# Sixteen extra score products behind the last block of exponentials, one shared step less, and a different instruction for epsilon

## The chip, the core and the metric

The kernel runs on one core of a Trainium2 chip. The metric is device time in microseconds (us) of one execution. Five engines work side by side, each on its own queue in its own order: TensorE (PE, its weight loads PEld), VectorE (DVE), ScalarE (ACT), GpSimd (POOL) and SyncE (SP, which here issues the transfers).

## The reference

Four batches of 12480 queries attend through 49 agents, and the result goes through a feed-forward layer with a cosine in it:

```python
def sm(a, b):
    s = scale * (a @ b.transpose(0, 2, 1))
    s = s - s.max(-1, keepdims=True)
    e = np.exp(s)
    return e / (e.sum(-1, keepdims=True) + 1e-09)
agent_v = sm(agents, k) @ v
x = (sm(q, agents) @ agent_v).reshape(B * S, D)      # 49920 x 128
h = x @ w_in                                          # 128 -> 2048
out = (h * np.cos(h)) @ w_out                         # 2048 -> 128
```

## The kernel before, in words

Queries are taken in 52 groups of 960 (13 a batch). The main loop (from L1115) has 832 steps, 16 a group and 208 a batch. A step n is one pair of 128-row tiles of the hidden layer for 480 queries. PE makes the pair `ph` from the turned weights `pT` and the folded weights `a` (two matmuls); ACT takes the cosine, `c<-ph`; DVE makes `r = (c - 1) * h` in one scalar_tensor_tensor, `r<-c,ph`; PE multiplies `r` by w_out into `po` four steps later (LAG = 4, L36). PSUM holds three `ph` pairs, one bank `po`, and one bank `one` for everything else. So the matmuls of `ph(n)` can only run when `r(n-3)` has been made, and every tile in `one` waits until the tile before it has been read.

Inside a step the instructions are issued in this order, and each engine keeps it: `ph(n)` on PE, the cosine on ACT, what `plan` holds for the step (L1133), `r(n)` on DVE, what `post` holds for the step (L1151), then the two `po` matmuls of step n-4 on PE. In every eighth step two more matmuls (`po<-pT,b`) go ahead of those, and ACT copies `po` to `osb` afterwards.

Beside this, the softmax of the queries is made ahead: PE makes their scores in `one` (`one<-ag,xt`, eight products of 120 queries by the 49 agents, given twice, so 98 columns; a product in fp32 appears as two passes in the trace), ACT the exponentials, DVE and POOL the sums, DVE adds epsilon and takes the reciprocal (`query_inverse`, L734), POOL multiplies (`p<-e,rz`), PE turns the result (`query_turned`, L746: four transposes into `one`, which ACT copies to `p`), and POOL splits it into `pT`.

Exponentials need another table on ACT than the cosine, so they are gathered in bursts (`burst`, L994): ACT loads a table, runs the exponentials, and loads the sine table again. In the last batch the burst stands behind the cosine of step 720 (T3 = 96, L70) and holds the last four groups. The steps 720 to 723 are shut to other jobs. The sums of three groups and their inverse follow at once on DVE; the sum of the fourth is made on POOL behind step 724 and its inverse behind step 729. `query_turned` of group 46 stands in step 724, in `plan`. `keep_warm` (L989) already exists: four score products with columns of `win` as weights, into a new tile in `one` that nobody reads; a count FB of zero (L95) issues none.

`asides` (L1105) names steps in which DVE does only the first half of `r`: ACT copies the second half of `h` to `raw`, and POOL makes that half of `r` in two instructions. In the last batch these are the steps whose number is 0 or 8 modulo 16, except near a burst.

Of the kernel before, what the change touches and what calls it, by code (L numbers as in the profile page):

```python
# [14 lines left out]
ALU = mybir.AluOpType  # L15
# [10 lines left out]
EPS = 1e-9  # L26
# [27 lines left out]
SR = 4  # L54
# [15 lines left out]
T3 = 96  # L70
# [7 lines left out]
PJ = 1  # L78
QI = 5
KQ = [2, 0, 1, 4, 2, 3, 3, 3, 1, 5, 2, 4, 0]  # L80
VQ = [2, 3, 4, 3, 3, 3, 3, 3, 3, 3, 3, 3, 3]
# [10 lines left out]
RB = 6  # L92
OG = 0
VP = 1
FB = 0  # L95
FO = 0
TS = 1
VX = [5, 6, 7, 8]
DW = 2
# [1 line left out]
P2 = 0  # L101
BL = 6
XL = 16
XP = []
XK = [0, 8]
# [17 lines left out]
EQ = [0, 1, 2, 3, 4, 5, 6, 7, 8, 9, 10, 11, 12]  # L123
# [10 lines left out]
def agent_attention_cos_ffn(ctx, tc, qT, kT, v, agT, w_in, w_out, outT):  # L134
    nc = tc.nc
    NB, _, N = qT.shape
# [5 lines left out]
    DFF = w_in.shape[1] - PAD // 2  # L142
    NF = DFF // P
    NP = NF // 2
    NG = N // GRP
# [11 lines left out]
    PER = NG * STEP  # L157
# [19 lines left out]
    pe, dve, act, pool = (Ordered(x) for x in (nc.tensor, nc.vector, nc.scalar, nc.gpsimd))  # L177
# [250 lines left out]
    class Fast(Agents):  # L428
# [64 lines left out]
        def projected(self, c, a, pw):  # L493
            cs = slice(c * 512, (c + 1) * 512)
            if c == 0:
                self.big = self.sb.tile([KR, DFF // 512], F32, name="big", bufs=1)
            act.activation(a[:, cs], pw[:KR], AF.Copy, scale=self.rz)
            x = a[:, cs].bitcast(F32)
            on = dve if self.wide else pool
            on.tensor_scalar(a[:, cs], x, 2 * FAST_MAX, -2 * FAST_MAX, op0=ALU.min, op1=ALU.max)  # L500
            if self.wide and BL:
                late_big.append((self, c, x))
            else:
                self.largest(c, x)
# [91 lines left out]
    with ExitStack() as pools:  # L596
# [15 lines left out]
        a = []  # L612
# [120 lines left out]

        def query_inverse(piece, i, j):  # L734
            rz = rz_of[piece][:, i * GT:j * GT]
            dve.tensor_scalar_add(rz, rz, EPS)
            dve.reciprocal(rz, rz)

        def query_weights(n, on=pool):
# [28 lines left out]
        ab = [Fast(sb, small, b) if b else First(sb, small, b, pair) for b in range(NB)]  # L768
# [5 lines left out]
        first = ab[0]  # L774
# [3 lines left out]
        def convert(n):  # L778

            for f in words[:n]:  # L780
                f()
            del words[:n]
# [59 lines left out]
        def wide_kept(n, ps):  # L842
            mx = sb.tile([TT, GT], F32, name="mx4", bufs=3)
            mh = mx.rearrange("p (h t) -> p h t", h=2)
            if QM == 0:
                dve.reduce_max(mh, ps, axis=AX.X)
                dve.tensor_sub(e_of[n].rearrange("p (h t) a -> p h t a", h=2), ps,
                               mh.unsqueeze(3).to_broadcast([TT, 2, HT, NA]))
                return
            dve.reduce_max(mh, ps, axis=AX.X)  # L850
            dve.tensor_scalar_mul(mx, mx, -SC)
            for h in range(2):
                for t in range(HT):
                    i = h * HT + t
                    act.activation(e_of[n][:, i], ps[:, h, t], AF.Exp, bias=mx[:, i:i + 1], scale=SC)
# [18 lines left out]
        piece = pieces[0]  # L874
# [48 lines left out]
            pe.matmul(po_v[:TT, :DC], qx[2][:, :TT], qx[2][:, :DC], start=True, stop=True)  # L923
        for n in range(3):
            wide_kept(n, outs[n])
        for g in range(NG):
            fetch_to(VL[g])
            shift(g + AH)
            if g + AH < NG:
                first.exp(g + AH, 1)  # L930
            first.add(g, dve if g in EQ else pool)
            first.values(g)
            convert(VQ[g])
            for c in range(4):
                if g == TQ[c]:
                    turn(c)
                if g == MQ[c]:
                    mult(c)
            if g == TW - 1 and QM == 0:
                for n in piece:  # L940
                    act.activation(e_of[n], e_of[n], AF.Exp, scale=SC)
            if g == TW:
                for n in piece:
                    query_sum(n)
                query_inverse(piece, 0, len(piece))
                query_weights(0, dve if PA else pool)
            if g == TR:
                query_turned(0, PA)
            if g == TI:
                first.total()  # L950
                first.inverse()
        sine_table()
        first.gather()
        if TI == NG:
            first.total()
            first.inverse()
        for c in range(4):
            if MQ[c] == NG:
                convert(len(words) if c == 3 else 0)
                mult(c)  # L960
# [10 lines left out]
        plan, post = Plan(), Plan()  # L971
# [22 lines left out]
        def burst(n, piece, two=(), ab=None, also=()):  # L994

            shut.update(range(n, n + SHUT))
            wide_at.update(range(n, n + SHUT + WX))
            for i in range(0, len(two), 2):
                post(n + i // 2 * BD, query_two, two[i:i + 2], piece_of[two[0]])
            if ab is not None:  # L1000
                for g, k in lots:
                    post(n, pinned_exp, ab, g, k)
            post(n, query_exp, piece)
            if also:
                post(n, query_exp, also)
                post(n + 12, query_sums, also, 0, len(also))
                post(n + 20, query_inverse, also, 0, len(also))
            s0 = SF if ab is not None else SD1
            for k in piece[:s0]:
                post(n, query_sum, k)  # L1010
            post(n, query_inverse, piece, 0, s0)
            m = n + SM
            if ab is not None:
                for k in piece[s0:]:
                    post(m, query_sum, k)
                    m += 1
                post(m, query_inverse, piece, s0, len(piece))
                return
            for i in range(s0, len(piece), ST):
                j = min(i + ST, len(piece))  # L1020
                post(m, query_sums, piece, i, j)
                m += 1
            post(m + SR, query_inverse, piece, s0, len(piece))

        for c in range(max(1, P2), DFF // 512):
            plan(PJ * (c - max(1, P2)), ab[0].project, c, a[0])
        def big_late():
            late_big[0][0].largest(*late_big.pop(0)[1:])
        if BL:
# [17 lines left out]
        for b in range(NB):  # L1047
            o = b * PER
            go, stop = o + (T1 if b < NB - 1 else T3), o + PER + T2
            last = OG and b == NB - 2  # L1050
            if OG and b == NB - 1:
                break
            k0 = o + (T2 + K0 if b else KB)
            spread_over(k0 + (QS if b < NB - 1 else 0), go - 5, go - 1, [q_lot(n) for n in early[b][N2 if b else N0:]])
            if b == NB - 1:
                burst(go, early[b])
                for i in range(FB):
                    post(go + FO, keep_warm)
                break
            nxt = ab[b + 1]  # L1060
            spread_over(k0, o + K1, o + K1 + 1, [[(nxt.scores, g, k) for k in range(2)] for g in range(NG)])
            plan(o + K1 + 2, nxt.top)
            job(o + K1 + 4, (nxt.across,), by=o + K1 + 5)
            job(o + K1 + 6, (nxt.spread,), by=o + K1 + 8)
            for g in range(NG):
                plan(o + K1 + 9 + SH * g, nxt.shift, g, 1, pool)
            burst(go, early[b], late[b][:N1], nxt)
            for g in range(0, NG, VP):
                at = go + V0 + (o + V1 - go - V0) * g / NG
                job(at, *((nxt.values, x, k) for x in range(g, min(g + VP, NG)) for k in range(2)), by=at + 6 * VP)  # L1070
            spread_over(go + QV, o + V1 + 8 if last else stop - 3, o + V1 + 8 if last else stop - 1, [q_lot(n) for n in late[b][N1:]])
            if last:
                spread_over(o + V1 + 6, stop - 1, stop - 1, [q_lot(n) for n in early[b + 1][:-2]])
                burst(stop, late[b], early[b + 1][-2:], also=early[b + 1])
            else:
                burst(stop, late[b], early[b + 1][:N2])
            i = (b + 1) % 2
            job(o + V1 + 3, (nxt.inverse,), by=o + V1 + 8)
            job(o + V1 + 6, *((nxt.project, c, a[i]) for c in range(DFF // 512)), by=o + PER - 6)
            job(o + V1 + 7, (nxt.project_out, wio, b1[i], b2[i]), by=o + PER + 2)  # L1080
# [8 lines left out]
        while queue or begun:  # L1089
# [7 lines left out]
            n, i, by, parts = x  # L1097
# [7 lines left out]
        def asides(n):  # L1105

            b, o = n // PER, n % PER
            if n < XA or n > NSTEP - 6 or any(x in shut for x in range(n - XB, n + XC)):
                return False
            if b == NB - 1:  # L1110
                return n % XL in XK
            return X0 <= o < X1 and n % XL in XP

        rs = {}
        for n in range(NSTEP + LAG):  # L1115
# [3 lines left out]
            if n < NSTEP:  # L1119
                q, c, i = n // STEP, n // NP % NCH, n % NP  # L1120
# [209 lines left out]
```

## Time and profile before

| what | us |
|---|---|
| median of three runs | 1174.71 (1174.52 to 1177.32) |
| the profiled execution | 1173.36 |
| its span, first to last instruction | 1171.6 |
| mean granted TensorE clock | 0.996 of full |

The span is 1.8 us shorter than the profiled execution's own time, which is 1.35 us under the median. In the profile, PE is TensorE's matmuls and PEld its weight loads. A row of the timeline merges neighbouring instructions of one kind (x is their count); in brackets is the idle time ahead of it and what ended it. Shapes are partitions x elements. Granted clock 1.00 is 2.4 GHz, 0.50 is 1.2 GHz.

### The profile page before, as it was taken

The numbers are of one execution on the slowest core, as the hardware profiler recorded it, in microseconds if no ns is written. First come the engines' busy times: TensorE is split into PE (matmuls) and PEld (weight loads), VectorE is DVE, ScalarE is ACT, GpSimd is POOL, SyncE is SP. The second block draws the span as 40 slices with busy tenths as digits, with TensorE's granted clock in tenths as the row PEclk, the third lists the DMA queues.
The fourth block names the chain that finished last, engine by engine and source line by source line (L and its number), as shares of the span: only waits on it lengthen the run. The fifth ranks groups of instructions, "written<-read, shape, count | busy, mean of one in ns | idle before, by whom it ended". The sixth has DMA issues, their size and how long they took to land.

```text
span 1171.6 us, 17200 instructions
## 1 busy us (share of the span) xinstructions
PE 1123.6 (96%) x6051; PEld 918.3 (78%) x6051; DVE 1063.3 (91%) x1202; ACT 979.4 (84%) x1268; POOL 566.7 (48%) x727
## 2 busy tenths in 40 slices
PE   9989999999999999999999999999999999989996
PEld 8869888778886898777887788877888667767774
DVE  5878888989998988989999998998999999989997
ACT  3567877889888878898888888898988999989996
POOL 2013313668963212639893331175896456545551
PEclk9999999999999999999999999999999999999998
DMA  8734333143331333133331333214331100000001
GB/s 327 306 125 134 117 119 102 51 138 106 106 105 51 102 116 104 51 102 106 106 106 52 96 105 104 91 45 138 106 98 59 35 18 34 34 18 34 17 34 38
DMA packets 31631, 109.44 MB, mean 93 GB/s; under 512 B 3504, under 2 KB 4016, under 8 KB 31536
## 3 DMA queue, kind: packets, MB, share of 16 engines
q1 hardware_dynamic: 31392, 108.13, 28.4%
q8 instruction: 50, 0.82, 0.3%
q14 instruction: 45, 0.37, 0.1%
q10 hardware_dynamic: 144, 0.12, 0.0%
HBM read 82.68 MB, written 25.56 MB: 92 GB/s over the span
## 4 chain that ended last, share of the span: by engine, by line
PE 60%; DVE 21%; ACT 13%; issue 5%; DMA 1%; POOL 0%; SPq 0%; ACTq 0%; DVEq 0%
PE ph L171 26%; PE po L171 22%; DVE r L171 15%; PE one L171 12%; ACT c L171 7%; ACT osb L171 1%; DVE rz L171 1%; ACT e L171 1%; ACT p L171 1%; ACT s L171 1%; DVE sums L171 1%; DVE e L171 1%; ACT L171 1%; DVE mx L171 1%; DMA c<-kT 1%
## 5 line engine op out<-in xcount | busy, mean ns | idle before, releaser
L171 DVE SCALAR_TENSOR_TENSOR r<-c,ph 128x960 fp32r<-128x960 f32 (+1 forms) x833 | 906.1, 1133 | 41.8 <-ACT c L171 35.3
L171 ACT ACTIVATE c<-ph 128x960 f32<-128x960 f32 x832 | 785.4, 977 | 140.5 <-PE ph L171 126.3
L171 PE MATMUL ph<-pT,a 113*128 113x480 f32 x1664 | 520.9, 394 | 21.6 <-DVE r L171 16.9
L171 PE MATMUL po<-r,w 128*128 128x480 f32 x1664 | 524.2, 396 | 5.6 <-ACT osb L171 5.4
L171 PEld LDWEIGHTS ph<-pT,a 113*128 113x128 f32 x1664 | 294.6, 189 | 137.5 <-DVE r L171 73.3
L171 PEld LDWEIGHTS po<-r,w 128*128 128x128 f32 x1664 | 292.6, 190 | 52.0 <-ACT osb L171 14.1
L171 POOL CAST pT<-p 49x480 fp32r<-49x480 f32 x102 | 59.4, 582 | 266.7 <-ACT p L171 263.9
L171 PEld LDWEIGHTS one<-ag,xt 128*120 128x120 f32 x1088 | 133.9, 184 | 12.0 <-DVE sums L171 1.4
L171 PE MATMUL one<-ag,xt 128*120 128x98 f32 x1088 | 134.4, 265 | 0.4 <-DVE b L171 0.2
L171 POOL TENSOR_TENSOR pT<-p,pT 49x480 fp32r<-49x480 f32 x102 | 124.3, 1219 | 8.2
L171 POOL TENSOR_TENSOR vh<-vt,vh 120x512 fp32r<-120x512 f32 x78 | 93.4, 1198 | 30.5 <-ACT vh L171 30.5
L171 POOL TENSOR_TENSOR p<-e,rz 120x392 f32<-120x392 f32 x51 | 43.7, 856 | 47.6 <-DVE rz L171 46.3
L171 PE MATMUL po<-pT,b 113*128 113x480 f32 x208 | 62.5, 381 | 0.0
L171 POOL TENSOR_TENSOR raw<-c,raw 128x480 f32<-128x480 f32 x24 | 29.6, 1231 | 67.5 <-ACT raw L171 67.4
L171 POOL TENSOR_TENSOR e<-e,mx 120x392 f32<-120x392 f32 x25 | 21.2, 847 | 84.7 <-DVE mx L171 84.7
L171 ACT COPY osb<-po 128x480 f32<-128x480 f32 x104 | 57.9, 557 | 2.2 <-PE po L171 2.2
L171 PEld LDWEIGHTS ph<-ag,xt 128*120 128x120 f32 x480 | 52.0, 185 | 7.3 <-DVE r L171 4.4
L171 PE MATMUL ph<-ag,xt 128*120 128x98 f32 x480 | 54.4, 269 | 2.7 <-DVE r L171 2.0
L171 PEld LDWEIGHTS one<-vh,eh 120*113 120x113 f32 x312 | 45.9, 177 | 8.3 <-POOL vh L171 2.5
L171 PE MATMUL one<-vh,eh 120*113 120x258 f32 x312 | 50.7, 284 | 1.4 <-DVE e L171 1.4
L171 POOL TENSOR_TENSOR eh<-s,eh 120x196 fp32r<-120x196 f32 x78 | 47.7, 612 | 6.3
L171 POOL CAST eh<-s 120x196 fp32r<-120x196 f32 x78 | 27.7, 355 | 32.7 <-ACT s L171 32.3
(135 smaller groups left out, 730.7 us busy)
## 6 DMA issues: line engine op xcount, KB each, us to landing
xt<-qT SPq DMA_DIRECT2D x52, 480.0 KB, 3.6
outT<-osb SPq DMA_DIRECT2D x51, 480.0 KB, 2.6
xt<-kT SPq DMA_DIRECT2D x46, 480.0 KB, 3.6
vt<-v SPq DMA_DIRECT2D x43, 512.0 KB, 3.7
c<-kT SPq DMA_DIRECT2D x6, 480.0 KB, 7.4
vh<-v SPq DMA_DIRECT2D x5, 512.0 KB, 6.7
raw<-w_in SPq DMA_DIRECT2D x2, 512.0 KB, 6.6
a<-w_in SPq DMA_DIRECT2D x2, 512.0 KB, 6.4
```

Of the source, the lines that this page charges most:

```text
L171: ins = f(*args, **kw)
```

## The change

New constants: FB = 4 and FO = 4 put four `keep_warm` behind step 720 + 4 of the last batch, 16 products, 32 passes in the trace. XZ = 12 takes the steps 720 to 731 out of `asides`; 720 was already out, being in the burst, so this is step 728 alone. EP = 1 makes `query_inverse` add epsilon by a scalar_tensor_tensor, max(rz + EPS, rz), in place of a tensor_scalar; it is called 17 times. The other new constants (AL, CV, SZ, TN, GF, PO, PK, BM) have the values at which their branches issue the same instructions in the same order as before: SZ equals SR, and TN equals TI.

```diff
-FB = 0
-FO = 0
+FB = 4
+FO = 4
+SZ = 4
+XZ = 12
+EP = 1
...
         def query_inverse(piece, i, j):
             rz = rz_of[piece][:, i * GT:j * GT]
-            dve.tensor_scalar_add(rz, rz, EPS)
+            if EP:
+                dve.scalar_tensor_tensor(rz, rz, EPS, rz, op0=ALU.add, op1=ALU.max)
+            else:
+                dve.tensor_scalar_add(rz, rz, EPS)
             dve.reciprocal(rz, rz)
...
             if b == NB - 1:
-                return n % XL in XK
+                return n % XL in XK and not T3 <= o < T3 + XZ
```

What issues the extra products was there already, in the setup of the last batch:

```python
burst(go, early[b])
for i in range(FB):
    post(go + FO, keep_warm)
```

## Rows read from the trace of the kernel before

**Rows 1.** The page: busy us of an engine, share of the span, instructions.
```profile
PE 1123.6 (96%) x6051; PEld 918.3 (78%) x6051; DVE 1063.3 (91%) x1202; ACT 979.4 (84%) x1268; POOL 566.7 (48%) x727
```
**Rows 2.** The page: the chain that ended last, shares by engine.
```profile
PE 60%; DVE 21%; ACT 13%; issue 5%; DMA 1%; POOL 0%; SPq 0%; ACTq 0%; DVEq 0%
```
**Rows 3.** Windows: stretch and its us, busy PE, PEld, DVE, ACT, POOL, clock, DMA.
```profile
1038.20:1041.78 3.58, 0.01 (x1) 0.00 (x0) 2.01 (x5) 3.55 (x5) 0.00 (x0) 1.00 0.00 0
1042.50:1045.90 3.40, 3.40 (x12) 2.91 (x12) 2.50 (x4) 2.51 (x4) 1.71 (x2) 0.50 0.36 145
...
1060.00:1160.00 100.00, 97.71 (x415) 71.91 (x414) 95.74 (x93) 95.07 (x121) 49.65 (x48) 1.00 0.08 33
```
**Rows 4.** Timeline of PE behind the last burst: start, us, engine, instruction.
```profile
1037.17 0.60 PE L171 MATMUL po<-pT,b 113*128 113x480 f32 x2
...
1041.78 0.71 PE L171 MATMUL ph<-pT,a 113*128 113x480 f32 x2 [3.58 <-DVE r L171]
...
1042.33 0.84 PE L171 MATMUL one<-ident,p 120*113 120x120 f32 x4
```
**Rows 5.** Timeline of ACT behind the last burst.
```profile
1043.44 0.60 ACT L171 COPY p<-one 113x480 f32<-113x480 f32 x1
1044.82 0.97 ACT L171 ACTIVATE c<-ph 128x960 f32<-128x960 f32 x1 [0.78 <-PE ph L171]
```
**Rows 6.** The chain in order of time: start, us, what, instructions merged.
```profile
1043.17 0.81 PE po L171 x2
1043.98 0.80 PE ph L171 x2
...
1047.11 0.44 PE po L171 x2
```
**Rows 7.** Timeline of PE in a step with eight score passes.
```profile
987.55 0.98 PE L171 MATMUL one<-ag,xt 128*120 128x98 f32 x8
988.32 0.68 PE L171 MATMUL po<-r,w 128*128 128x480 f32 x2
```
**Rows 8.** Timeline of DVE behind the last burst, and one later period.
```profile
1045.82 1.15 DVE L171 SCALAR_TENSOR_TENSOR r<-c,ph 128x960 fp32r<-128x960 f32 x1 [0.90 <-ACT c L171]
1047.27 2.87 DVE L171 SCALAR_TENSOR_TENSOR r<-c,ph 128x960 fp32r<-128x960 f32 x3 [0.29 <-ACT c L171]
1050.36 1.16 DVE L171 SCALAR_TENSOR_TENSOR r<-c,ph 128x960 fp32r<-128x960 f32 x1 [0.22 <-ACT c L171]
1051.43 0.28 DVE L171 TENSOR_SCALAR rz<-rz 120x8 f32<-120x8 f32 x1
...
1068.32 8.46 DVE L171 SCALAR_TENSOR_TENSOR r<-c,ph 128x960 fp32r<-128x960 f32 x8 [0.22 <-ACT c L171]
```
**Rows 9.** Tile rz: count, least/median/most ns, first and last start.
```profile
L171 DVE TENSOR_SCALAR rz<-rz x17: 172/178/875, 50.3 to 1051.4; 120x24 f32<-120x24 f32 x13, 120x32 f32<-120x32 f32 x3, 120x8 f32<-120x8 f32 x1
```
**Rows 10.** Timeline of POOL and DVE, one slow epsilon of three like it.
```profile
254.41 1.20 POOL L171 TENSOR_TENSOR pT<-p,pT 49x480 fp32r<-49x480 f32 x1
254.78 0.87 DVE L171 TENSOR_SCALAR rz<-rz 120x24 f32<-120x24 f32 x1
```
**Rows 11.** Groups of DVE by form: count, busy us, mean ns, idle before.
```profile
L171 DVE SCALAR_TENSOR_TENSOR r<-c,ph 128x960 fp32r<-128x960 f32 x807 | 889.2, 1149 | 38.6 <-ACT c L171 35.3
...
L171 DVE SCALAR_TENSOR_TENSOR r<-c,ph 128x480 fp32r<-128x480 f32 x26 | 16.9, 654 | 3.1 <-ACT raw L171 0.7
...
L171 DVE TENSOR_SCALAR rz<-rz 120x24 f32<-120x24 f32 x13 | 4.4, 337 | 0.3
...
L171 DVE TENSOR_SCALAR rz<-rz 120x32 f32<-120x32 f32 x3 | 1.0, 338 | 0.0
```
**Rows 12.** Timeline of POOL and DVE in the first part.
```profile
50.98 1.20 POOL L171 TENSOR_TENSOR p<-e,rz 120x392 f32<-120x392 f32 x1 [43.29 <-DVE rz L171]
51.40 1.21 DVE L171 TENSOR_TENSOR s<-s,mxb 120x392 f32<-120x392 f32 x1
```
**Rows 13.** Tile s, 0 to 70 us: count, least/median/most ns.
```profile
L171 DVE TENSOR_TENSOR s<-s,mxb x13: 552/560/1206, 31.6 to 58.8; 120x392 f32<-120x392 f32 x13
```

More of the change, by code (lines that the diff above doesn't have):

```diff
@@ L94 @@
 VP = 1
-FB = 0
-FO = 0
+FB = 4
+FO = 4
+AL = 0
+CV = 0
+SZ = 4
+XZ = 12
+TN = 12
+GF = 1
+PO = 0
+PK = 0
+BM = 0
+EP = 1
 TS = 1
@@ L500, in projected @@
             on.tensor_scalar(a[:, cs], x, 2 * FAST_MAX, -2 * FAST_MAX, op0=ALU.min, op1=ALU.max)
-            if self.wide and BL:
+            if BL if self.wide else BM:
                 late_big.append((self, c, x))
@@ L925, in agent_attention_cos_ffn @@
             wide_kept(n, outs[n])
+        added = 0
         for g in range(NG):
@@ L930, in agent_attention_cos_ffn @@
                 first.exp(g + AH, 1)
-            first.add(g, dve if g in EQ else pool)
+            while added < min(NG, g + 1 + (AL if g else 0)):
+                first.add(added, dve if added in EQ else pool)
+                added += 1
             first.values(g)
-            convert(VQ[g])
+            if not (CV and g == NG - 1):
+                convert(VQ[g])
             for c in range(4):
@@ L950, in agent_attention_cos_ffn @@
                 first.total()
+            if g == TN:
                 first.inverse()
         sine_table()
-        first.gather()
+        if GF:
+            first.gather()
         if TI == NG:
             first.total()
+        if TN == NG:
             first.inverse()
+        if not GF:
+            first.gather()
+        if CV:
+            convert(VQ[NG - 1])
         for c in range(4):
@@ L1022, in burst @@
                 m += 1
-            post(m + SR, query_inverse, piece, s0, len(piece))
+            post(m + (SR if n < T3 + (NB - 1) * PER else SZ), query_inverse, piece, s0, len(piece))
         for c in range(max(1, P2), DFF // 512):
-            plan(PJ * (c - max(1, P2)), ab[0].project, c, a[0])
+            (post if PO >> c & 1 else plan)(PJ * (c - max(1, P2)) + (PK >> c & 1), ab[0].project, c, a[0])
         def big_late():
@@ L1052, in agent_attention_cos_ffn @@
                 break
+            if BM and b:
+                for c in range(DFF // 512):
+                    post(o + BM + 3 * c, big_late)
             k0 = o + (T2 + K0 if b else KB)
```

## The prediction
> **What bounds the kernel now.** I read the page first: PE is busy for 96% of the span [rows 1], but the chain that ended last gives PE only 60% and DVE 21% [rows 2]. So a busy PE is not yet the engine that sets the pace, and the pace has to be read stretch by stretch. The change touches two kinds of places: the stretch behind the last burst, and the 17 calls that add epsilon.
>
> The windows of that stretch come next [rows 3]. From 1038.20 to 1041.78 PE does nothing: ACT has loaded its table, run four exponentials and loaded the sine table again, and is making the first cosines, while the three `ph` pairs wait to be read. Then PE resumes at full clock, and from 1042.5 to 1045.9 it runs at the granted clock 0.50 (1.2 GHz); outside this stretch the clock is full until the end of the computation. PE is 100% busy in the slow stretch, DVE and ACT are not: 2.50 and 2.51 of 3.40 us. Here PE is the bound. Later, from 1060 to 1160, PE, DVE and ACT are all busy for over 95%, and nothing that was lost can be made up.
>
> The timeline says where in PE's order the new passes come. The matmuls `po<-pT,b` at 1037.17 belong to product step 719, issued in loop step 723, so the `ph` that waited 3.58 us and started at 1041.78 is that of step 724 [rows 4]. Behind it stand the four transposes of `query_turned`, which are in `plan` of step 724. The new passes are in `post` of the same step: behind both, ahead of `po(720)` and of `ph(725)`.
>
> **The 32 passes.** A removed or added instruction on PE between 1041.78 and 1046 moves the end, since DVE and ACT wait for `ph` there: ACT's cosine of step 725 waited 0.78 us for it [rows 5], and DVE's `r(725)` then 0.90 us for the cosine [rows 8].
>
> First their start. They write into `one`, which the transposes have filled and which ACT's copy to `p` reads from 1043.44 to 1044.04 [rows 5]. Before, PE went on at 1043.17 with `po(720)` [rows 6]; now it waits until 1044.04, and 0.04 more for the signal, 0.91 us in all, with `po(720)` and `ph(725)` queued behind.
>
> Then their length. Eight passes of the same shape took 988.32 - 987.55 = 0.77 us [rows 7], 0.096 us each at full clock; 32 take 3.08 us. At the slow clock a pair of matmuls took 0.81 us where it takes 0.44 later [rows 6], a factor of 1.8, so 0.175 us a pass. I take the slow stretch to end where it ended before, at 1045.9: (1045.90 - 1044.08) / 0.175 = 10.4 passes in it, and 21.6 x 0.096 = 2.07 us for the rest, until 1047.97. Then `po(720)` and `ph(725)`, 0.44 us each [rows 6] and 0.02 to ACT: the cosine of step 725 starts at 1048.87 instead of 1044.82 [rows 5], 4.05 us later. DVE's `r(725)`, next in line, starts as much later, at 1049.87.
>
> What comes back: the second gap of DVE in the slow stretch, 0.29 us [rows 8], since everything behind is at full clock. The first gap, 0.90 us, is only replaced by a longer one. Nothing is ahead of time that could take up the rest: DVE has made `r(724)` by 1044.92, 0.90 us ahead of `r(725)` [rows 8], and has no other work whose turn has come, as its next small job stands behind `r(729)`. Together 4.05 - 0.29 = +3.76 us.
>
> Bounds of this term: all passes at full clock end at 1044.08 + 3.08 = 1047.16, which is 0.81 us less, +2.95; all at half clock end at 1044.08 + 5.6 = 1049.68, and `po(720)` and `ph(725)` then take 0.8 us each [rows 6]: the cosine at 1051.3, 6.5 us later, less the gap +6.2. I take the middle because PE works on after its resumption as it did before, except for the 0.91 us.
>
> **The step that is no longer shared.** In step 728 DVE now makes the whole of `r`. The stretch with that step took 2.87 us for two whole and one half, and 0.22 us of idle time followed, in which DVE waited for a cosine [rows 8], because ACT's copy had delayed it: 3.09 us for three steps. Eight steps with one shared one take 8.46 + 0.22 = 8.68 us [rows 8], 1.085 a step, so three whole steps take about 3.26: +0.17 us. Bounds: +0.5 us if the idle time stays (654 ns against 1149 ns [rows 11]), and 0 if sharing saves nothing, as 1.085 a step already suggests. POOL and ACT lose three instructions that nobody was waiting for. One of them, POOL's product for the shared half, stood in the way of epsilon at 1051.43, which took 0.28 us [rows 8] instead of 0.17 [rows 9]: -0.10 us.
>
> **Epsilon by another instruction.** Undisturbed, the tensor_scalar takes 172 to 178 ns [rows 9]. A scalar_tensor_tensor of 24 elements isn't in the trace. From the two lengths of `r`, (1149 - 654) / 480 = 1.03 ns an element and a fixed 159 ns [rows 11], so an estimate of 184 ns: no difference that counts, 0.1 us over all 17.
>
> What could count is the disturbed ones. At 254.78 epsilon took 0.87 us; it started while POOL was at `pT<-p,pT` and ended with it [rows 10]. The form of 24 elements sums to 13 x (337 - 178) = 2.07 us of such waiting (three calls of 0.69) and that of 32 to 3 x (338 - 174) = 0.49 us [rows 11]. That is 2.56 us, and all of it lies between two `r` on DVE without a gap, so it is on the path.
>
> Does the new instruction escape it? The nearest row is a DVE instruction with two tensor inputs in SBUF: `s<-s,mxb` at 51.40 came while POOL ran `p<-e,rz`, and took 1.21 us [rows 12] where its median is 0.56 [rows 13]. The `r` instructions, which have one input in PSUM, don't stretch beside POOL. The new instruction reads `rz` twice, both from SBUF, so I count its wait like that of `s<-s,mxb`: 0 gained. The other end is -2.56 us. The row is of another operation and of two different tensors, so it does not settle it. The Trainium skill (SBUF — State Buffer, Who interferes with whom) says it in general: a DVE instruction with two SBUF inputs contends with a GpSimd instruction that reads SBUF, and the second to issue blocks until the first is done. By that rule the exchange gives nothing, and the sum is the one below; an instruction that escaped would be a rival.
>
> **The sum.** +3.76 + 0.17 - 0.10 + 0.1 = +3.9 us, made against the profiled execution: 1173.36 becomes 1177.3. That execution is 1.35 us under the median of the runs, to which I add the same: 1174.71 + 3.9 = 1178.6 us.
>
> **The rivals.**
>
> Slow clock stays on. PE now stands still for 0.91 us inside the slow stretch, and all the passes run at 1.2 GHz. For it: the clock fell at 1042.5, after 3.58 us in which PE did nothing [rows 3]. Against it: 0.91 us is far less, and no other stretch of the main loop with short PE gaps lost the clock. By the upper bound +6.2 + 0.2 = +6.4: 1181.1 us.
>
> Epsilon escapes POOL. The four long waits go: 3.9 - 2.56 = +1.3, 1176.0 us. For it: reading one tensor twice isn't what [rows 12] shows. Against it: both reads are from SBUF all the same.
>
> The passes fall into PE's idle time, the other side. If they ran ahead of `ph(724)`, they would use 3.08 of the 3.58 us in which PE had nothing to do [rows 3, 7]; they would cost nothing, PE would not have stood still, and with a full clock the gaps of 0.90 and 0.29 us [rows 8] would go: -1.2 + 0.2 = -1.0, 1173.7 us. It is decided by whether the first pass starts before 1041.78. For it: the passes fit. Against it: by the order of issue they stand behind `ph(724)`, which itself waits for `r(721)`, and behind transposes whose tile they need.
>
> **How the numbers follow.** No change is less than 0.3%, 3.5 us, about what a measurement can tell here; the three runs alone lie 2.8 us apart. My forecast has 0.48; since 3.9 us is just above the bound, 0.33 of it counts as slower and 0.15 as the same. The slow clock that stays has 0.16, all slower. Epsilon that escapes has 0.21, of it 0.19 the same and 0.02 slower. Idle time used has 0.10: 0.06 the same and 0.04 faster. The other 0.05 I give to things not thought of, all faster. Together faster 0.09, same 0.40, slower 0.51. The range goes from a little below the escaping epsilon, 1174.8, to the slow clock that stays, 1181.2; it leaves out the idle time used and what was not thought of.
>
> **What would show it.** In the changed kernel's timeline: passes `one<-ag,win` on PE that start only after ACT's copy to `p`, some 2.3 us after the first `ph` behind the burst; an idle PE of about 0.9 us ahead of them; the cosine of step 725 almost 5 us behind the end of that copy; a slow stretch of about 3.4 us as before; epsilon as a scalar_tensor_tensor with three calls still at 0.8 us or more; no copy `raw<-ph` in step 728. I am wrong if the first pass stands ahead of the `ph` that waited, if the long epsilons are gone, or if DVE's gap behind `r(724)` is under 3 us.

## The result, and the profile after

The changed kernel takes 1183.62 us (median of 10 runs, 1181.21 to 1186.97); the kernel before, run beside it, 1176.08 us (10 runs, 1173.67 to 1180.12). The ratio is 1.0069, 95% interval 1.0057 to 1.0082: slower by 8.1 us (0.0069 x 1176.08), where 3.9 was forecast and 1181.2 was the top of the range. The direction was right, the size was not.

The two profiled executions differ by more, 1185.21 - 1173.36 = 11.85 us. I split them at three instructions of DVE: `r(0)`, the first `r` of the main loop; `r(721)`, the first behind the last burst; and `r(737)`, behind the next shared half step.

| stretch | before, us | after, us | difference |
|---|---|---|---|
| start to r(0) | 73.54 | 77.18 | +3.64 |
| r(0) to r(721) | 967.03 | 967.18 | +0.15 |
| r(721) to r(737) | 19.08 | 27.14 | +8.06 |
| r(737) to the end of the span | 111.9 | 111.9 | 0.0 |

The 8.06 us are the change. The 3.64 us are not: they lie in the setup, where the change touches one epsilon of 0.2 us, and they go with a fall of the clock there that some traces have and others lack (experiment e11). The kernel before happened to be profiled without that fall, the changed one with it; this is why the two profiles differ by more than the medians.

The windows of the changed kernel show the places: us, then busy time of PE, PEld, DVE, ACT, POOL, the granted clock, DMA.

```profile
67.20:77.40 10.20, 8.33 (x19) 4.81 (x20) 1.93 (x8) 2.94 (x5) 0.00 (x0) 0.50 0.24 97
1041.99:1045.57 3.58, 0.00 (x1) 0.01 (x1) 2.02 (x5) 3.55 (x5) 0.00 (x0) 1.00 0.00 0
1046.81:1057.05 10.24, 9.00 (x36) 8.05 (x37) 1.89 (x2) 1.02 (x2) 6.43 (x12) 0.50 0.13 50
...
1064.00:1164.00 100.00, 97.70 (x413) 71.53 (x412) 95.75 (x94) 95.10 (x121) 48.34 (x46) 1.00 0.08 30
```

The idle time behind the burst is the same 3.58 us, and from 1064 on everything is as before [rows 3]. But the stretch at 1.2 GHz lasts 10.24 us where it lasted 3.4, and DVE and ACT are busy for 1.89 and 1.02 us of it.

PE's timeline, to be held against [rows 4] and [rows 6], shows the passes where the order of issue put them:

```profile
1045.57 0.70 PE L181 MATMUL ph<-pT,a 113*128 113x480 f32 x2 [3.58 <-DVE r L181]
1046.10 0.58 PE L181 MATMUL one<-ident,p 120*113 120x120 f32 x4
1047.88 7.86 PE L181 MATMUL one<-ag,win 128*120 128x98 f32 x32 [1.20 <-ACT p L181]
1055.44 1.15 PE L181 MATMUL po<-r,w 128*128 128x480 f32 x2
1056.38 0.91 PE L181 MATMUL ph<-pT,a 113*128 113x480 f32 x2
```

They wait 1.20 us for ACT's copy of the transposes, start 2.31 us behind the first `ph`, and `po(720)` starts 7.56 us later. The weight loads and the chain in order of time show stops inside: each new tile begins with one, and the tiles follow each other every 1.98 us.

```profile
1049.86 1.68 PEld L181 LDWEIGHTS one<-ag,win 128*120 128x120 f32 x8 [0.30 <-PE one L181]
```
```profile
1047.88 1.93 PE one L181 x8
1049.81 0.04 issue
1049.86 1.94 PE one L181 x8
```

DVE's timeline, against [rows 8], shows what that costs:

```profile
1044.36 4.35 DVE L181 SCALAR_TENSOR_TENSOR r<-c,ph 128x960 fp32r<-128x960 f32 x4 [1.49 <-ACT c L181]
1058.34 5.41 DVE L181 SCALAR_TENSOR_TENSOR r<-c,ph 128x960 fp32r<-128x960 f32 x5 [9.64 <-ACT c L181]
1063.67 0.16 DVE L181 SCALAR_TENSOR_TENSOR rz<-rz 120x8 f32<-120x8 f32 x1
...
1071.50 5.53 DVE L181 SCALAR_TENSOR_TENSOR r<-c,ph 128x960 fp32r<-128x960 f32 x5 [0.22 <-ACT c L181]
```

The gap ahead of `r(725)` is 9.64 us instead of 0.90: 8.74 us. Of these 0.68 come back up to `r(737)`: among others the gap of 0.29 us is gone, and epsilon, now undisturbed, takes 0.16 us. Epsilon elsewhere, against [rows 9] and [rows 11]:

```profile
L181 DVE SCALAR_TENSOR_TENSOR rz<-rz x17: 159/184/878, 50.7 to 1063.7; 120x24 f32<-120x24 f32 x13, 120x32 f32<-120x32 f32 x3, 120x8 f32<-120x8 f32 x1
```
```profile
L181 DVE SCALAR_TENSOR_TENSOR rz<-rz 120x24 f32<-120x24 f32 x13 | 4.4, 342 | 0.3
```

The longest still takes 878 ns, and three of the 13 take 0.87 us or more; the mean of 13 went from 337 to 342.

### The profile page after: what moved, and what is told of

Same layout as the page of the kernel before. It is cut to its first block, busy times and chain, and to the rows that moved or that the text cites. A ratio compares the mean times of both kernels' runs of the same rounds, so it can differ in the third digit from the quotient of the medians.

```text
span 1183.4 us, 17259 instructions
## 1 busy us (share of the span) xinstructions
PE 1135.0 (96%) x6083; PEld 926.5 (78%) x6083; DVE 1063.3 (90%) x1202; ACT 979.4 (83%) x1267; POOL 564.2 (48%) x725
## 4 chain that ended last, share of the span: by engine, by line
PE 60%; DVE 20%; ACT 13%; issue 4%; DMA 1%; POOL 0%; SPq 0%; ACTq 0%; DVEq 0%
PE ph L181 27%; PE po L181 21%; DVE r L181 15%; PE one L181 12%; ACT c L181 7%; DVE rz L181 2%; ACT osb L181 1%; ACT p L181 1%; ACT e L181 1%; DVE e L181 1%; DVE sums L181 1%; DMA c<-kT 1%; DVE mx L181 1%; ACT s L181 1%; DMA xt<-qT 1%
## 5 line engine op out<-in xcount | busy, mean ns | idle before, releaser
L181 PEld LDWEIGHTS po<-pT,b 113*128 113x128 f32 x208 | 38.7, 188 | 6.0
```

What stands on the lines that cost most here:

```text
L181: ins = f(*args, **kw)
```

## The experiments

All edits are to the changed kernel, except e2. For each I read the gap ahead of `r(725)` on DVE (0.90 us before, 9.64 in the changed kernel), the stretch at 1.2 GHz behind the burst (3.4 and 10.2), and the time from `r(721)` to `r(737)` against the 19.08 us before, worked out from the starts of those two in DVE's timeline. These hold whatever the setup did in that run.

| kernel | gap, us | slow stretch, us | r(721) to r(737), against before | ratio of times (95%) |
|---|---|---|---|---|
| the change | 9.64 | 10.2 | +8.06 | 1.0069 (1.0057 to 1.0082) |
| e1, no passes | 0.70 | 3.4 | -0.33 | 0.9992 (0.9977 to 1.0006) |
| e2, passes alone | 9.82 | 13.7 | +9.35 | 1.0072 (1.0047 to 1.0097) |
| e3, passes a step earlier | 0.18 | none | -0.34 | 0.9992 (0.9978 to 1.0005) |
| e4, 8 passes | 3.78 | 6.8 | +2.73 | 1.0014 (0.9999 to 1.0029) |
| e5, 16 long matmuls | 9.35 | 10.2 | +7.77 | one run |
| e6, ahead of the transposes | 9.23 | 13.7 | +8.50 | one run |
| e9, passes in one tile | 7.07 | 6.8 | +5.49 | one run |
| e10, long ones in one tile | 7.35 | 6.8 | +5.77 | one run |

**e1, no passes.**
```diff
-FB = 4
+FB = 0
```


> The changed kernel without the 32 passes; epsilon by the new instruction and step 728 whole, as in the change. Theory A (the passes are the whole loss): 0.998 to 1.002 of before; behind the burst the start of r(725) is where it was before, and r(737) within 0.4 us of it. The four long epsilons stay at 0.65 to 0.88 us. Theory B (the new epsilon or the step costs part of the loss): 1.002 or more, and the distance between the two kernels' r grows at an epsilon or between steps 726 and 737.

Ratio 0.9992. DVE's timeline and the window of its slow stretch:
```profile
1044.30 4.35 DVE L181 SCALAR_TENSOR_TENSOR r<-c,ph 128x960 fp32r<-128x960 f32 x4 [1.49 <-ACT c L181]
1049.35 1.16 DVE L181 SCALAR_TENSOR_TENSOR r<-c,ph 128x960 fp32r<-128x960 f32 x1 [0.70 <-ACT c L181]
1050.96 4.35 DVE L181 SCALAR_TENSOR_TENSOR r<-c,ph 128x960 fp32r<-128x960 f32 x4 [0.45 <-ACT c L181]
```
```profile
1046.70:1050.10 3.40, 3.40 (x9) 2.77 (x9) 2.70 (x3) 2.19 (x4) 2.12 (x3) 0.50 0.36 145
```
A: without the passes nothing is lost, and the slow stretch is 3.4 us as before. The whole `r` of step 728 costs nothing: `r(726)` to the next epsilon takes 4.26 us here (1050.96 to 1055.22) and 4.16 before with a shared half [rows 8], and the disturbed epsilon gives 0.12 back.

**e2, the passes alone**, in the kernel before:
```diff
-FB = 0
-FO = 0
+FB = 4
+FO = 4
```


> The kernel before with the 32 passes and nothing else. Theory A (the passes are the whole loss): ratio 1.006 to 1.008, r(725) 8.7 us later against before, r(737) 8.1 us later, the slow stretch behind the burst about 10 us instead of 3.4. Theory B (part of the loss is of the other edits): 1.004 or less.

Ratio 1.0072, A. The slow stretch was even longer, 13.7 us, and `r(737)` came 9.35 us later against before, where 8.1 was expected:
```profile
1044.04:1057.70 13.66, 12.78 (x48) 11.03 (x47) 3.84 (x4) 3.43 (x6) 5.62 (x11) 0.50 0.09 37
```
The shared step 728 was there, and epsilon ran into POOL's second instruction for it, 0.66 us where the changed kernel needs 0.16.

**e3, the passes one step earlier**, so that they stand ahead of `ph(724)`, which waits for `r(721)`:
```diff
-FO = 4
+FO = 3
```


> The changed kernel with the 32 passes issued one step earlier (step 723), ahead of the first-layer matmuls that wait behind the burst. Theory A (a pass costs 0.20 us only because the clock is already at 1.2 GHz when it runs): the passes take 0.096 us each and some 0.15 to 0.26 us at each of three changes of tile, 3.5 to 3.9 us in all, fill the idle time of PE, no slow stretch follows the burst, and r(725) starts 0.5 to 1.2 us earlier against before; ratio 0.998 to 1.001. Theory B (these passes are slow by themselves, with weights of win or tiles that nobody reads): 7.5 us again, the waiting matmuls of step 724 start some 4 us late and r(725) 3 to 5 us late; ratio 1.003 or more.

```profile
1038.86 4.39 PE L181 MATMUL one<-ag,win 128*120 128x98 f32 x32
...
1043.03 0.68 PE L181 MATMUL po<-pT,b 113*128 113x480 f32 x2
...
1043.99 0.61 PE L181 MATMUL ph<-pT,a 113*128 113x480 f32 x2
```
```profile
1038.86:1046.00 7.14, 6.97 (x49) 6.13 (x48) 5.46 (x9) 6.87 (x11) 0.00 (x0) 1.00 0.07 25
```
```profile
1046.99 5.41 DVE L181 SCALAR_TENSOR_TENSOR r<-c,ph 128x960 fp32r<-128x960 f32 x5 [0.18 <-ACT c L181]
1052.57 0.79 DVE L181 SCALAR_TENSOR_TENSOR rz<-rz 120x8 f32<-120x8 f32 x1 [0.17 <-POOL rz L181]
```
The same 32 passes take 4.17 us here (1038.86 to 1043.03) against 7.56, the clock stays at 2.4 GHz, and no slow stretch follows. So it is the place, not the passes. They take a little longer than expected and make `ph(724)` half a microsecond late (1043.99, while `r(721)` started at 1042.25 and such an `r` takes 1.15 us). `r(725)` starts 4.74 us behind `r(721)` instead of 5.25, and the next gap of 0.29 us is gone: 0.8 us won. Epsilon then waits 0.79 us behind POOL, which has come to `p<-e,rz` just then, and the gain is mostly taken. A for the mechanism; the ratio is that of e1.

**e4, a quarter of the passes.**
```diff
-FB = 4
+FB = 1
```


> The changed kernel with 8 passes instead of 32, in the same place. Theory A (the clock stays low because of the many passes that run at 1.2 GHz): 1.2 us of waiting and 8 x 0.20 = 1.6 us of passes, the slow stretch ends after about 3.4 us as before, r(725) 2.8 us late. Theory B (the standstill of 1.2 us ahead of the passes is what keeps the clock low): the slow stretch is about 10 us here too, steps then take 1.6 us instead of 1.08 for some six steps, r(737) 5 to 6 us late.

```profile
1045.97 1.92 PE L181 MATMUL one<-ag,win 128*120 128x98 f32 x8 [0.74 <-ACT p L181]
1047.59 1.15 PE L181 MATMUL po<-r,w 128*128 128x480 f32 x2
```
```profile
1044.15:1050.97 6.82, 6.08 (x22) 5.16 (x22) 3.04 (x4) 2.74 (x4) 4.54 (x6) 0.50 0.18 72
```
Neither fits: 0.74 us of waiting and 1.62 us of passes, and a slow stretch of 6.8 us, twice that without passes. The loss, 2.73 us, is what A expected, but the clock came back later than A said. Which property of the extra work holds it low was open; e5, e6, e9 and e10 ask that.

**e5, other work of the same length in the same place.**
```diff
-            ps = small()[:TT, :(GT + 1) * NA].rearrange("p (t a) -> p t a", a=NA)
+            ps = small()[:, :CH]
             for t in range(HT):
-                pe.matmul(ps[:, t:t + 2], win[:, t * TT:(t + 1) * TT], twice(ag[:, 0]), start=True, stop=True)
+                pe.matmul(ps, a[1][:, t * P:(t + 1) * P], pTs[0][:, 0], start=True, stop=True)
```


> The changed kernel with the 32 short passes replaced by 16 matmuls of 480 columns (the folded weights and a finished pT of the same batch as operands) in the same place and the same four tiles: 3.5 us at the full clock, 6.4 us at 1.2 GHz. Theory A (it is the short passes that the clock does not come back from): the slow stretch is about 3.4 us, as without passes, although PE stands still just as long ahead of them; the matmuls take 4 to 5.5 us and r(725) is 5.5 to 6.5 us late. Theory B (the standstill ahead of them, or any extra work there, keeps the clock low): the slow stretch is 6.8 us or more, and r(725) 7.5 us late or more.

```profile
1042.45:1052.69 10.24, 9.36 (x23) 6.32 (x22) 2.81 (x3) 2.02 (x4) 6.46 (x12) 0.50 0.12 48
```
```profile
1046.57 1.30 PEld L181 LDWEIGHTS one<-pT,a 113*128 113x128 f32 x4 [0.72 <-PE one L181]
```
B: matmuls of 480 columns, like those that the loop itself runs, kept the clock low just as long. My theory that it takes short passes does not hold in this execution. The weight loads show 0.72 us without a load at each change of tile.

**e6, the passes without the wait for ACT.**
```diff
-                    post(go + FO, keep_warm)
+                    plan(go + FO, keep_warm)
```


> The changed kernel with the 32 passes in the same step, but ahead of the four transposes, so that their tile is free and PE does not wait for ScalarE's copy. Theory A (the short passes keep the clock low): no idle time of PE ahead of them, and yet a slow stretch of 6.8 us or more; r(725) 6 to 8.5 us late. Theory B (the standstill keeps it low): the slow stretch is about 3.4 us, the passes take 5 to 5.5 us, r(725) 4.5 to 5.5 us late.

```profile
1043.70 1.17 PE L181 MATMUL ph<-pT,a 113*128 113x480 f32 x2 [3.58 <-DVE r L181]
1044.66 7.71 PE L181 MATMUL one<-ag,win 128*120 128x98 f32 x32
1052.52 1.11 PE L181 MATMUL one<-ident,p 120*113 120x120 f32 x4
```
```profile
1043.67:1057.32 13.65, 13.30 (x48) 11.57 (x49) 4.29 (x4) 3.90 (x6) 2.81 (x4) 0.50 0.09 37
```
There is no idle time ahead of the passes, and the slow stretch is as long as in e2, the longest of all. In this execution the clock stayed low without the standstill.

**e9 and e10, one tile**, so that no change of tile stops PE: all 16 products go into one. In e10 the same is done with the 16 long matmuls of e5 (its edit is not shown).
```diff
-FB = 4
+FB = 1
-            for t in range(HT):
+            for t in [*range(HT)] * 4:
```


> The changed kernel with the same 32 passes, all into one tile, so that the three stops of 0.26 us at changes of tile are gone. Theory A (the stops keep the clock low): the slow stretch is 6.8 us or less, and r(725) at most 6.5 us late. Theory B (the passes themselves do, as they leave the array idle while weights are loaded): 10 us or more again, the passes take 32 x 0.20 = 6.4 us, r(725) 7.5 to 8.2 us late.

> The 16 matmuls of 480 columns in place of the passes, all into one tile. With stops at changes of tile they kept the clock low for 10.2 us. Theory A (the stops do it): the slow stretch is 3.4 or 6.8 us, the matmuls take 4.5 to 6 us, r(725) 6 to 7 us late. Theory B (the standstill of 0.7 to 1.2 us ahead of them does it, in whatever work follows): 10 us, the matmuls take 6.4 us, r(725) 7.3 us late or more.

PE's passes in e9, and the windows of the slow stretch in e9 and in e10:
```profile
1044.88 5.95 PE L181 MATMUL one<-ag,win 128*120 128x98 f32 x32 [0.72 <-ACT p L181]
```
```profile
1043.03:1049.85 6.82, 6.10 (x31) 5.72 (x30) 2.67 (x3) 1.80 (x4) 4.53 (x6) 0.50 0.19 74
```
```profile
1044.11:1050.94 6.83, 5.63 (x16) 4.62 (x15) 2.13 (x3) 1.25 (x2) 4.98 (x8) 0.50 0.18 72
```
A in both, but for e10's matmuls, which took 6.1 us where A had at most 6: 6.8 us instead of 10.2, for short passes and long matmuls alike. The four traces with changes of tile behind the burst (the change, e2, e5, e6) have 10.2 or 13.7 us, the three whose extra work goes into one tile (e4, e9, e10) 6.8. In e9 the clock came back while the passes were still running (at 1049.85; they end at 1050.83), so it is not only that there was less left to run. The stops at changes of tile are thus a likely part of what kept the clock low, but this is not shown: each kernel was traced in one execution, and the same 32 passes gave 10.2 us once and 13.7 another time. The rest of the delay, from 3.4 to 6.8 us, stays in every kernel with extra work behind the `ph` that waited. What the clock asks for remains open.

**e7, no epsilon.**
```diff
-FB = 4
+FB = 0
...
-            if EP:
-                dve.scalar_tensor_tensor(rz, rz, EPS, rz, op0=ALU.add, op1=ALU.max)
-            else:
-                dve.tensor_scalar_add(rz, rz, EPS)
             dve.reciprocal(rz, rz)
```


> The changed kernel without the passes and without the addition of epsilon (left out: 1e-9 added to sums that are at least 1, as the largest exponential is 1). Theory A (DVE's waits at epsilon are on the path): against the run without passes 3 to 5 us are gone, some 0.7 to 0.9 us at each of the four long ones and 0.2 at most of the others; ratio to before 0.995 to 0.997. Theory B (the wait moves to the next instruction, or another engine is late): under 1.5 us, ratio 0.998 or more.

Ratio to before 0.9969 (0.9956 to 0.9981). From `r(0)` to `r(721)` it takes 963.69 us, and e1 967.25: 3.56 us are gone, 2.5 of them at the four long epsilons (0.53 to 0.71 us at each, a little less than expected). A: the waits were on the path, and they don't move to the next instruction:
```profile
L181 DVE RECIPROCAL rz<-rz 120x24 f32<-120x24 f32 x13 | 3.9, 301 | 0.3
```
The mean of these was 303 ns before. At 261.39 such a reciprocal took 0.30 us while POOL was at `pT<-p,pT` (261.01 to 262.21), the same neighbour that held epsilon up for 0.69 us. So reading `rz` in SBUF is not enough to wait for POOL: the tensor_scalar and the scalar_tensor_tensor did, the reciprocal did not.

**e8 and e11, the two gains together.** e8 is e7 with 24 passes in the place of e3 (FB = 3, FO = 3). e11 adds 16 passes in the setup, where PE waits for DVE's sums:
```diff
             if g == TN:
+                for _ in range(2):
+                    keep_warm()
                 first.inverse()
```


> Without the addition of epsilon (as in the run with that name), and with 24 passes in step 723, ahead of the matmuls that wait. The 32 passes there took 4.2 us and made the waiting matmuls 0.5 us late; 24 should take 3.1 us and delay nothing. If both gains add: no slow stretch behind the burst, r(737) 1.0 to 1.4 us earlier against the kernel without epsilon and passes, ratio to before 0.994 to 0.996. If the clock's gain is taken up by another wait as with 32 passes: within 0.4 us of the kernel without epsilon and passes.

> The kernel without epsilon and with 24 passes ahead of the waiting matmuls, and with 16 more passes in the first part, where PE waits 2.3 us for VectorE's sums at 65 us. In seven of nine traces of other kernels so far the clock fell at 67 to 70 us, for 3.4 or 10.2 us, and r(0) came 1.6 to 6 us later than in the two without. Theory A (the passes there hold the clock): no slow stretch before 100 us, r(0) at 73.5 to 74.2 us, the runs scatter less and the median is 1168.5 to 1169.8, ratio 0.993 to 0.995. Theory B (the fall has another cause, or the passes delay the sums' product): r(0) at 75 us or later, median as without them, 1170.4 or more.

e8: ratio 0.9955 (0.9940 to 0.9970), median 1170.37 us (1168.51 to 1174.87). The 24 passes are through in 3.3 us, `ph(724)` is on time, and no slow stretch follows:
```profile
1034.06 3.26 PE L181 MATMUL one<-ag,win 128*120 128x98 f32 x24
...
1037.46 9.79 DVE L181 SCALAR_TENSOR_TENSOR r<-c,ph 128x960 fp32r<-128x960 f32 x9 [1.71 <-ACT c L181]
```
`r(721)` to `r(737)` takes 17.59 us, in e7 18.77; in this stretch the gains add. e11: ratio 0.9939 (0.9923 to 0.9955), median 1168.93 us, and its runs lie within 0.8 us (1168.43 to 1169.22). In its setup PE's gap is filled, the clock stays up, and `r(0)` starts at 73.75:
```profile
65.18 2.14 PE L181 MATMUL one<-ag,win 128*120 128x98 f32 x16
67.66 0.33 PE L181 MATMUL one<-ones,e 120*113 120x1 f32 x2 [0.34 <-DVE e L181]
```
```profile
65.00:80.00 15.00, 11.72 (x61) 7.34 (x59) 9.21 (x20) 8.53 (x13) 0.00 (x0) 1.00 0.34 133
```
A. All twelve traces without these passes have a gap of 2.3 us there. In seven of them the clock fell at 67 to 70 us and `r(0)` came at 75.1 to 80.1 (in e7, the latest, the clock had also fallen once before); in the other five (the kernel before, e5, e8, e9, e10) it did not fall, and `r(0)` came at 73.5 to 74.8. The expectation's count of nine and two is too low. One trace of e11 without a fall could therefore be luck. What speaks against luck is that all six runs of e11 have a mean clock of 0.997 or 0.998, but only six of e8's twelve. e11 has the lowest median here, 14.7 us below that of the change; its interval overlaps that of e8.

## Why the prediction was right in direction and wrong in size

Right: the place of the passes in PE's order, the wait for ACT's copy (first pass forecast 2.30 us behind the waiting `ph`, measured 2.31), that DVE and ACT have nothing to make the loss up with, and that epsilon by a scalar_tensor_tensor waits for POOL just the same (the longest 878 ns, before 875). The Trainium skill (SBUF — State Buffer, Who interferes with whom) has this rule for any DVE instruction with two SBUF inputs beside a GpSimd instruction that reads SBUF; the trace agrees, with 878 ns where the median is 184. e7 bears out that these waits are on the path. e1 and e2 show that the passes alone are the loss. PE's idle time ahead of the passes was 1.20 us and not 0.91, since the transposes ran at full clock here and ended sooner; the start of the passes did not move by it, as ACT's copy sets it.

Wrong is the step "I take the slow stretch to end where it ended before, at 1045.9". It ended 11.5 us after the first `ph` behind the burst, not 4.1. The end was taken from the trace of the kernel without the passes. The term of the passes was mis-sized in three ways, which the traces of the change and of e4 separate:

- Forecast were 3.89 us from the first pass to `po(720)` (1044.08 to 1047.97), measured 7.56 (1047.88 to 1055.44). A pass at 1.2 GHz takes 0.20 us (1.62 us for eight in e4), not 0.175: 32 of them 6.4 us. I had scaled by a pair of 480 columns, which slows down by 1.8; the passes slow down by 0.20 / 0.096 = 2.1. Why the two differ is not shown.
- Three changes of tile take 1.98 - 8 x 0.20 = 0.38 us each, 1.1 us in all, which I had at nothing: the weight loads of each new tile wait 0.30 us for PE's own last matmul on the tile before, which lies in the same bank, though nobody reads it.
- `po(720)` and `ph(725)` then ran at 1.2 GHz too, from 1055.44 until the cosine at 1057.33: 1.89 us, forecast 0.90.

Together 3.67 + 0.99 = 4.66 us more than the 4.05 forecast for the cosine, which gives the 8.7 us by which `r(725)` is late.

The rival of the slow clock that stays on is what happened, in its outcome. I gave it 0.16, because PE was to stand still for only 0.91 us. In e6 the clock stayed low without this standstill, so the reason that I weighed, for and against, is not what decides it; e9 and e10 point to the stops between tiles as one cause, and the rest stays open. Its price, +6.4, lacked 0.8 us for the passes and 1.1 for the changes of tile: with them 8.3, where 8.06 were measured.

The smaller terms were about right: step 728 was forecast at +0.17 and the last epsilon at -0.10; e1 shows +0.10 and -0.12. The idle time as a place for the passes, my rival on the other side, is real: e3 is it, one step of issue away. Its price, -1.0, was too high: e3 gained 0.34 us, no more than e1, as epsilon's wait for POOL took up most of the rest.

## What to carry to other kernels

Work that is to hold the clock belongs where the engine would be idle, that is, ahead of the instruction that waits (e3, e8, e11). Behind that instruction it ran at the low level here, delayed what waited, and the level stayed low two to four times as long. Write such filler into one tile (5.49 us lost in e9 against 8.06), and read the stretch's granted clock in the trace of the kernel with the filler, not in that of the kernel without it. When a small DVE instruction waits for GpSimd, exchanging it for another may change nothing: here the tensor_scalar waited, and so did the scalar_tensor_tensor that reads the same tensor twice. Leaving it out ended the wait (e7).

## What the runs showed of the hardware that I had not expected

- The clock did not come back under extra matmuls that keep PE busy: in e6 PE was busy for 13.30 of 13.65 us at 1.2 GHz, while in e1 the clock came back after 3.4 us of the loop's own work.
- A new tile in the same PSUM bank cost PE 0.38 us at 1.2 GHz, without any reader in between.
- A reciprocal with one input in SBUF took its usual 0.30 us beside a POOL instruction that made a tensor_scalar and a scalar_tensor_tensor on the same tile wait for up to 0.7 us.
- A fall of the clock in the setup, behind the same gap of 2.3 us in seven of twelve traces and not in the other five, makes `r(0)` start at 75.1 to 80.1 us instead of 73.5 to 74.8. It probably explains most of the scatter of the runs: with 16 passes in that gap the six runs of e11 lie within 0.8 us, without them the twelve of e8 within 6.4.
